# Eighteen unread matrix products behind the last useful one, in five layouts and two widths of weights

## The chip, the core and the metric

The kernel runs on one core of one Trainium2 chip. A core has five engines with instruction streams of their own: PE (TensorE, matrix products into PSUM), DVE (VectorE), ACT (ScalarE), POOL (GpSimd) and SP (SyncE, which here issues most of the DMAs and closes the program). They wait for each other through semaphores. The metric is the device time of one execution in microseconds (us), as the median of some runs.

## The reference

Two blocks follow each other. The first is a linear attention with a polynomial sketch; the second is a feed-forward block with a gate.

```python
phi(x) = outer(S1 @ x, S2 @ x)             # 8 x 8 = 64 features of each token
kv  = sum over s of phi(k) v               # per batch and head
z   = sum over s of phi(k)
x   = (phi(q) @ kv) / (phi(q) @ z + 1e-6)  # 4 batches, 4 heads, 1088 tokens, 32 wide
g   = x @ w_gate                           # x laid out as 4352 tokens x 128
out = (g * sigmoid(g) * (x @ w_val)) @ w_out   # 128 -> 1536 -> 128
```

## The kernel before

The feed-forward block works on transposed tokens: columns are tokens, and the 1536 hidden features are twelve tiles of 128 rows (`j` from 0 to 11). Tokens come in blocks, most of them 480 wide; the last one, `LAST`, is 384 wide and is cut in two for its down projection, 256 columns (`SPLIT`) that go the usual way and 128 that go "straight".

Products in full fp32 are dear on PE, and part of the work is therefore done in *exact parts*. A factor is cut by `cut_weights`, `cut_tokens`, `cut_down` and `cut_hidden` into a high part and a scaled low part that the faster type `float32r` holds without loss; a product of full numbers then becomes three products of parts (L989, L1001 and L1002 for the two up projections, L1069, L1071 and L1072 for the down projection). In the trace a product in full fp32 is two matmul records with a weight load each; a product of exact parts is one. `w_parts[id(wg), 3]` holds the parts of the gate's weights for tiles 9 to 11, and `down_parts["w1"]`, ten tiles of 128 columns, the high parts of the down weights.

PSUM has eight banks of 512 fp32 columns, in one tile `PS`. Single banks are named `g0`, `g1`, `g2` and `acc` (banks 0 to 3), and two pairs `a` (4 and 5) and `b` (6 and 7); `wide("b")` returns the latter pair as a 128 x 2 x 512 view.

The order on each engine is the order in which the code is written; no scheduler moves anything. The main loop goes over the units `(block, j)`: `start_unit` (L989, with an ACT pass at L992), `finish_unit` (L1001, L1002, the activation at L1004, the multiplication on DVE at L1009) and, some units behind, `down`. After the loop PE has left what the last block still owes: the rest of `down` (L1077, in full fp32, negated weights `scaled`) with, in between, twelve `straight` products (L1117, full fp32, 128 x 128, summed in bank 4). Then DVE copies that sum to `o_last` (L1430), and four DMAs, two issued by SP and two by ACT, store it (L1436). Another store, of the other 256 columns (L1141), goes out just before.

What ends the program stands under the line of the function's end, L1462. SP waits there for each DMA queue's last landing and for the engines' last results that it has not yet seen, two semaphores to an instruction; then all engines meet in a barrier, in which POOL collects a signal from each, and in a second one. PE has only its drain and the barrier to do behind its last product.

Of the kernel before, what the change touches and what calls it, by code (L numbers as in the profile page):

```python
# [19 lines left out]
def kernel(  # L20
# [28 lines left out]
    nc = tc.nc  # L49
    P = nc.NUM_PARTITIONS  # L50
# [46 lines left out]
    def touch(*which):  # L97
        for i in which:
            clock[0] += 1
            used[i] = clock[0]  # L100
# [11 lines left out]
    def bank(tag=None):  # L112

        if tag is not None:
            i = place[tag]
        else:
            i = place[free_banks[turn[0] % len(free_banks)]]
            turn[0] += 1
        touch(i)
        return PS[:, i, :]  # L120
# [17 lines left out]
    def wide(tag):  # L138
        i = place[tag]
        touch(i, i + 1)  # L140
        return PS[:, i : i + 2, :]
# [8 lines left out]
    wg = const.tile([P, NCH, P], FP32, name="wg")  # L150
# [84 lines left out]
    def keep_warm(n, w=TB, ps=None):  # L235


        if ps is None:
            ps = bank(free_banks[turn[0] % len(free_banks)])
        for _ in range(n):  # L240
            nc.tensor.matmul(
                ps[0:32, 0:w], warm[:, 0:32], warm[:, 0:w], start=True, stop=True
            )
# [570 lines left out]
    w_parts = {}  # L814
# [76 lines left out]
    down_parts = {}  # L891
# [162 lines left out]
    def down(y=None):  # L1054

        i, j = todo.pop(0)
        n = SPLIT if i == LAST else blocks[i][1]
        first = i not in acc
        if first:
            acc[i] = bank("g2" if i == 1 or i in line[2::2] else "acc")  # L1060
        made[i] = made.get(i, 0) + 1
        mine = [c for c in range(NCH) if (i, c) in DOWN]
        if mine and j == mine[0]:
            acc[i, "p"] = bank("acc" if i in line[2::2] else "g2")
        sides = dict(start=first, stop=(made[i] == NCH))
        if j in mine:
            w1, wb, wd = [down_parts[x][:, FINE.index(j), :] for x in ("w1", "wb", "wd")]
            h1, h0, hd = h_parts.pop((i, j))
            nc.tensor.matmul(acc[i][:, 0:n], wd, hd, **sides)  # L1069
            p = acc[i, "p"][:, 0:n]  # L1070
            nc.tensor.matmul(p, w1, h1, start=(j == mine[0]), stop=False)  # L1071
            nc.tensor.matmul(p, wb, h0, start=False, stop=(j == mine[-1]))  # L1072
            if j == mine[-1]:
                copy_out(y, i, n)
        else:
            w = down_parts["scaled"][:, PLAIN.index(j), :] if mine else wo[:, j, :]
            nc.tensor.matmul(acc[i][:, 0:n], w, hidden[i, j][:, 0:n], **sides)  # L1077
        if i != LAST:
            hidden.pop((i, j))
            slots.append(slot_of[i, j])  # L1080
        if made[i] == NCH:
            if mine:
                put_together(y, i, n)
            elif i == HEAD - 1:

                add_to(behind, 1, lambda: store(i, n))
            else:
                store(i, n)
# [26 lines left out]
    def straight(ps, j):  # L1115

        nc.tensor.matmul(  # L1117
            ps,
            hidden.pop((LAST, j))[:, SPLIT : SPLIT + P],
            wo[:, j, :],  # L1120
            start=(j == 0),
            stop=(j == NCH - 1),
        )
# [3 lines left out]
    def store(i, n):  # L1127
# [7 lines left out]
        while t0 < t1:  # L1135
# [8 lines left out]
                )  # L1144
            t0 += 32 * m

    keep_warm(98, 32)
    keep_warm(12, 64)
    fills = {(w, i): narrow_w(w, i) for w in weights for i in range(len(pieces[w]))}
# [14 lines left out]
    for h in range(H):  # L1164
# [4 lines left out]
            start=True,  # L1169
            stop=True,  # L1170
# [30 lines left out]
    n = steps[0][1]  # L1201
# [95 lines left out]
    w = ("wg", "wv")  # L1297
# [127 lines left out]
    for j in range(NCH):  # L1425
        if todo and j % 4 == 0:
            down()
        straight(ps, j)
    o = fpool.tile([P, D], FP32, name="o_last")
    nc.vector.tensor_copy(o[:], ps)  # L1430
    t0 = blocks[LAST][0] + SPLIT
    b, x0 = divmod(t0 // 32, NX)
# [34 lines left out]
```

## Time and profile before

| | us |
|---|---|
| median of 3 runs (lowest to highest) | 276.84 (276.68 to 276.86) |
| the profiled execution: span from first to last instruction | 275.1 |
| PE busy | 268.8 (98%) |
| VectorE busy | 214.1 (78%) |
| ScalarE busy | 193.6 (70%) |
| GpSimd busy | 105.7 (38%) |
| mean granted TensorE clock | 0.999 |

The profile has no other time of its own execution than the span; what lies around the span, 1.7 us against the median, is the start and the end of an execution outside of the instructions. In a row such as `271.88 0.29 DVE L1430 COPY`, the numbers are the start from the span's beginning and the duration, in us. Records of PE's matmuls overlap, since each holds the time through the array: what a matmul costs its successor is the distance between two starts, not the duration. Rows of groups end in the busy time in us, the mean of one in ns, and the idle time before them.

### The profile page before, as it was taken

To read this page: it belongs to the slowest core of one execution; us is meant where nothing else is said; L and a number is where in the kernel's file an instruction comes from. 1 tells how busy PE (TensorE), PEld (TensorE's weight loads), DVE (VectorE), ACT (ScalarE), POOL (GpSimd) and SP (SyncE) were. 2 spreads that over 40 slices of the span, in tenths; PEclk is the share of its full clock that TensorE was granted. 3 is DMA by queue.
4 is the path that set the end of the run, shared out by engine and by line. 5 is a ranking of instruction groups with operands and counts; after the bars stand their busy time and mean duration, and the time that the engine had idled before them with its cause. 6 is when DMAs were issued, how large, how long until landed. Compare 5 with 4: busy or idle time off the path is not lost.

```text
span 275.1 us, 5788 instructions
## 1 busy us (share of the span) xinstructions
PE 268.8 (98%) x2191; PEld 200.5 (73%) x2191; DVE 214.1 (78%) x373; ACT 193.6 (70%) x349; POOL 105.7 (38%) x117
## 2 busy tenths in 40 slices
PE   7999999999999999999999999999999999999995
PEld 6645566666785786777577777867887888789994
DVE  3997988989788773887545766967987995998871
ACT  2468666462685686677479898769879888897880
POOL 3313422149350640260034353435535663553330
PEclk9999999999999999999999999999999999999999
DMA  6573196122231043000200020000100200010021
GB/s 191 172 216 87 49 270 200 60 104 62 62 88 23 4 111 99 2 0 0 38 12 4 1 38 0 0 2 11 26 2 0 36 1 0 13 25 1 2 36 29
DMA packets 26139, 14.30 MB, mean 52 GB/s; under 512 B 19840, under 2 KB 24192, under 8 KB 26112
## 3 DMA queue, kind: packets, MB, share of 16 engines
q1 hardware_dynamic: 25456, 13.84, 19.6%
q8 instruction: 17, 0.28, 0.4%
q10 hardware_dynamic: 656, 0.10, 0.2%
q14 instruction: 10, 0.08, 0.1%
HBM read 11.41 MB, written 2.23 MB: 50 GB/s over the span
## 4 chain that ended last, share of the span: by engine, by line
PE 93%; DVE 3%; DMA 2%; ACT 1%; issue 0%; SPq 0%
PE PS L1077 20%; PE PS L1001 14%; PE PS L989 14%; PE PS L1002 14%; PE PS L1025 12%; PE PS L1072 3%; PE PS L1071 3%; PE PS L1069 3%; PE PS L354 2%; PE PS L776 2%; PE PS L342 2%; DMA kld<-in_k_dram 2%; PE PS L388 2%; PE PS L1117 1%; PE PS L497 1%; PE PS L445 1%
## 5 line engine op out<-in xcount | busy, mean ns | idle before, releaser
L992 ACT ACTIVATE PS<-PS 128x960 f32<-128x960 f32 (+1 forms) x90 | 83.3, 926 | 29.8 <-PE PS L989 28.8
L1009 DVE SCALAR_TENSOR_TENSOR hbuf<-PS,sg 128x480 f32<-128x480 f32 (+1 forms) x87 | 55.2, 634 | 36.6 <-ACT sg L1004 36.1
L1004 ACT ACTIVATE sg<-PS 128x480 f32<-128x480 f32 (+1 forms) x90 | 49.6, 551 | 1.6 <-PE PS L1002 1.2
L1077 PE MATMUL PS<-hbuf,wo 128*128 128x480 f32 (+2 forms) x94 | 39.4, 516 | 0.0
L989 PE MATMUL PS<-xd,graw 128*128 128x480 f32 (+1 forms) x69 | 37.5, 543 | 0.0
L989 PE MATMUL PS<-xd,wd 128*128 128x480 f32 (+1 forms) x90 | 33.6, 373 | 0.0
L1002 PE MATMUL PS<-x,wb 128*128 128x480 f32 (+1 forms) x90 | 33.5, 372 | 0.0
L1001 PE MATMUL PS<-x,w 128*128 128x480 f32 (+1 forms) x90 | 33.4, 371 | 0.0
L1002 PE MATMUL PS<-x,graw 128*128 128x480 f32 (+1 forms) x69 | 25.5, 370 | 0.0
L989 PEld LDWEIGHTS PS<-xd,wd 128*128 128x128 f32 x90 | 17.0, 189 | 9.9 <-issue 5.3
L1025 PE MATMUL PS<-xT,wg 128*128 128x384 f32 (+1 forms) x60 | 23.5, 473 | 0.1
L1025 PE MATMUL PS<-xT,wv 128*128 128x384 f32 (+1 forms) x60 | 23.2, 467 | 0.3 <-DVE wv L286 0.3
L868 POOL TENSOR_TENSOR x<-xT,x 128x480 fp32r<-128x480 f32 (+1 forms) x6 | 7.2, 1195 | 37.8 <-ACT x L865 37.8
L1077 PEld LDWEIGHTS PS<-hbuf,wo 128*128 128x128 f32 x94 | 17.7, 189 | 5.4 <-issue 0.4
L1029 ACT ACTIVATE sg<-PS 128x384 f32<-128x384 f32 (+1 forms) x24 | 11.2, 468 | 13.2 <-PE PS L1025 12.4
L969 POOL TENSOR_TENSOR hlate<-hbuf,hlate 128x480 fp32r<-128x480 f32 (+1 forms) x12 | 14.6, 1218 | 11.0 <-ACT hlate L968 9.7
L989 PEld LDWEIGHTS PS<-xd,graw 128*128 128x128 f32 x69 | 13.0, 188 | 7.6 <-ACT PS L992 4.1
L1001 PEld LDWEIGHTS PS<-x,w 128*128 128x128 f32 x90 | 16.9, 187 | 2.2
L1002 PEld LDWEIGHTS PS<-x,wb 128*128 128x128 f32 x90 | 16.9, 188 | 2.1
L1001 PE MATMUL PS<-x,graw 128*128 128x480 f32 (+1 forms) x48 | 18.1, 376 | 0.0
L1077 PE MATMUL PS<-hbuf,scaled 128*128 128x480 f32 (+1 forms) x40 | 17.1, 518 | 0.0
L1025 PEld LDWEIGHTS PS<-xT,wv 128*128 128x128 f32 x60 | 11.2, 190 | 7.4 <-DVE hbuf L1040 0.8
(205 smaller groups left out, 572.0 us busy)
## 6 DMA issues: line engine op xcount, KB each, us to landing
kld<-in_k_dram SPq DMA_DIRECT2D x4, 544.0 KB, 4.4
vld<-in_v_dram SPq DMA_DIRECT2D x12, 144.0 KB, 4.3
qld<-in_q_dram SPq DMA_DIRECT2D x3, 544.0 KB, 4.8
raw<-in_moe_w_out_dram SPq DMA_DIRECT2D x4, 384.0 KB, 4.4
raw<-in_moe_w_gate_dram SPq DMA_DIRECT2D x3, 384.0 KB, 3.3
raw<-in_moe_w_val_dram SPq DMA_DIRECT2D x3, 384.0 KB, 3.5
out_dram<-o SPq DMA_DIRECT2D x16, 60.0 KB, 2.0
vld<-in_v_dram SPq DMA_DIRECT2D x4, 112.0 KB, 4.1
```

The lines of the kernel that those rows point to most:

```text
L969: add_to(before, y + 2, lambda: nc.gpsimd.tensor_tensor(out=h0, in0=h, in1=whole(h1), op=ALU.subtract))
L989: nc.tensor.matmul(ps[:, k], w_parts[id(w), j // 3][2][:, j % 3, :], xd, start=True, stop=True)
L992: nc.scalar.activation(ps, ps, AF.Copy, scale=-1.0 / WHOLE)
L1001: nc.tensor.matmul(ps[:, k], w1, x1, start=False, stop=False, skip_group_check=True)
L1002: nc.tensor.matmul(ps[:, k], wb, x0, start=False, stop=True, skip_group_check=True)
L1004: nc.scalar.activation(sg, ps[:, 0], AF.Silu, scale=WHOLE)
L1009: nc.vector.scalar_tensor_tensor(out=hj[:, 0:n], in0=ps[:, 1], scalar=WHOLE, in1=sg, op0=ALU.mult, op1=ALU.mult)
L1025: nc.tensor.matmul(o[:, 0:n], w[:, j, :], xT[:, t0 : t0 + n], start=True, stop=True)
L1029: nc.scalar.activation(sg[:, 0:n], g[:, 0:n], AF.Silu)
L1069: nc.tensor.matmul(acc[i][:, 0:n], wd, hd, **sides)
L1071: nc.tensor.matmul(p, w1, h1, start=(j == mine[0]), stop=False)
L1077: nc.tensor.matmul(acc[i][:, 0:n], w, hidden[i, j][:, 0:n], **sides)
```

## The change

A new function `behind_all` is called between the last `straight` product and the copy to `o_last`. It issues eighteen products of exact parts on PE. The weights are always the high parts of one tile of the gate's weights, the moving operand is always 256 columns out of `down_parts["w1"]`. Each of six views is used three times in a row: the first 256 columns; 256 columns from the second one on; every second one of 512 columns; the first 256 columns taken in steps of 16; the first column 256 times; and again the first 256 columns, with 32 columns of weights in place of 128. The sums alternate between banks 6 and 7, always 256 contiguous columns, and nobody reads them. The output of the kernel is the same.

```diff
+    def behind_all():
+
+        n = 256
+        unread = wide("b")
+        w = w_parts[id(wg), 3][0][:, 0, :]
+        x = down_parts["w1"].rearrange("p c d -> p (c d)")
+        views = [
+            x[:, 0:n],
+            x[:, 1 : n + 1],
+            x[:, 0 : 2 * n].rearrange("p (c t) -> p t c", t=2)[:, 0],
+            x[:, 0:n].rearrange("p (c t) -> p t c", t=16),
+            x[:, 0:1].to_broadcast([P, n]),
+            x[:, 0:n],
+        ]
+        for k, view in enumerate(views):
+            m = 32 if k == 5 else P
+            o = unread[0:m, k % 2, 0:n]
+            if k == 3:
+                o = o.rearrange("p (t c) -> p t c", t=16)
+            for _ in range(3):
+                nc.tensor.matmul(o, w[:, 0:m], view, start=True, stop=True)
 
     keep_warm(98, 32)
     keep_warm(12, 64)
...
         if todo and j % 4 == 0:
             down()
         straight(ps, j)
+    behind_all()
     o = fpool.tile([P, D], FP32, name="o_last")
     nc.vector.tensor_copy(o[:], ps)
     t0 = blocks[LAST][0] + SPLIT
```

## The prediction

> **What bounds the kernel now.** I read the page's first two parts, then the chain that ended last, then the timeline of the last microseconds, and last the instructions of the closing line L1462, by narrow windows.
>
> ```profile
> span 275.1 us, 5788 instructions
> PE 268.8 (98%) x2191; PEld 200.5 (73%) x2191; DVE 214.1 (78%) x373; ACT 193.6 (70%) x349; POOL 105.7 (38%) x117
> PEclk9999999999999999999999999999999999999999
> ```
>
> PE (TensorE) is busy 98% of the span at full granted clock. So work put into its stream before its last useful product would cost its own duration. The change puts work behind that product, so the end has to be read by itself. The chain and the timeline there:
>
> ```profile
> 269.62 0.43 PE PS L1077 x2
> 270.05 1.80 PE PS L1117 x16
> 271.88 0.29 DVE o_last L1430
> ```
> ```profile
> 271.12 0.72 PE L1117 MATMUL PS<-wo,hbuf 128*128 128x128 f32 x5
> 271.88 0.29 DVE L1430 COPY o_last<-PS 128x128 f32<-128x128 f32 x1 [0.88 <-PE PS L1117]
> 272.19 0.80 SPq L1436 DMA_DIRECT2D out_dram<-o_last  x2
> 272.20 0.84 ACTq L1436 DMA_DIRECT2D out_dram<-o_last  x2
> ```
>
> The last product ends at 271.84, VectorE starts its copy 0.04 later, and the four stores are issued until 273.04. From there PE has nothing to do. What the program's end waits for:
>
> ```profile
> DMA to landing us min/median/max: 1.4/1.5/1.6
> L1462 SPq EVENT_SEMAPHORE  x1: 28/28/28, 274.2 to 274.2; - x1
> L1462 PEldq DRAIN  x2: 13/1210/2408, 269.5 to 274.8; - x2
> SPq L1462 <- DMA out_dram<-o_last: 0.8, 2, 0.5
> ```
>
> The first line is of the L1436 stores, the other three are of the closing line. SyncE sits until the stores have landed; the wait that is released last starts at 274.23 (nothing of L1462 stands between 273.95 and 274.23). From there to the end, 275.11, there is only the closing barrier, 0.88 us. PE's first drain, its ticket to that barrier, was over 2.41 us after 269.5, at 271.9. So between 271.84 and about 274.2 PE is free: the cover of this change.
>
> **The change part by part.** Eighteen matmuls with their weight loads are added to PE behind L1117; nothing is removed or moved. In the built order PE has no new wait, VectorE's copy still waits for the twelfth product of L1117 alone, and the DMAs stand as before. One wait is new: SyncE's closing waits now include PE's eighteenth product, sharing an instruction with the landing of a store (the one at 274.23); that splits the eleven waits over one instruction more. The additional one stands first, where SyncE waits for landings anyway: 0 while that cover holds, and one event, some 0.06 by the spacing of these waits, without it. Instruction loading: the page counts 17 blocks, the trace shows about 255 PE instructions between the last blocks and 147 after the last one; 36 more stay inside it, so 0.
>
> Banks 6 and 7 are free and never read. VectorE's copy of bank 4 (0.29) now runs while PE writes other banks, which is also so for every L1009 evacuation: 0; were it to double, the stores would be 0.29 later.
>
> So the only question is when the eighteenth product ends. The plain price, from six such products (exact parts, 256 columns, 128 weights):
>
> ```profile
> 264.10 0.28 PE L1069 MATMUL PS<-hqld,dparts 128*128 128x256 f32 x1
> 264.21 0.28 PE L1071 MATMUL PS<-hkld,dparts 128*128 128x256 f32 x1
> 264.57 0.28 PE L1071 MATMUL PS<-hqld,dparts 128*128 128x256 f32 x1
> 264.69 0.28 PE L1072 MATMUL PS<-hvld,dparts 128*128 128x256 f32 x1
> ```
>
> From 264.10 to 264.69 are five steps: 0.118 each, 0.46 ns a column. The first new product can start 0.112 (the step of L1117) after the last old one started (271.56), at 271.68. All at the plain price: the eighteenth starts 17 x 0.118 = 2.01 later, at 273.69, ends 0.28 later, at 273.97, and its semaphore is seen 0.04 later, at 274.01. That is 0.22 us before 274.23. **Cover left: 0.22 us.**
>
> Layouts, three products each:
> - *Plain, and all from one column (step 0)*: plain price. Step 0 touches less than plain does. Bounds 0.118 and, if a product of exact parts fell back to the price of a full fp32 product, 0.43 (two instructions of 0.215, from six L1077 instructions at 256 columns in 1.29).
> - *Start one column late*: the same contiguous run, 0.118; the same upper bound.
> - *32 weights of 128*: the same columns stream. The sums over ones, L401, use 32 weights and take 379 ns at 256 columns, as L1077 does with 128 weights. So 0.118, upper bound 0.43.
> - *Step 2 and step 16 (8 and 64 bytes between columns)*: no PE row reads with a step. The nearest rows are VectorE's:
>
> ```profile
> L277 DVE SCALAR_TENSOR_TENSOR man<-raw,man 128x384 f32<-128x384 uint32 x10 | 5.5, 549 | 0.0
> L748 DVE TENSOR_TENSOR qab<-qab,den 128x288 f32<-128x288 f32 x3 | 1.4, 457 | 0.1
> L744 DVE TENSOR_REDUCE den<-dot 128x36 f32<-128x288 f32 x3 | 1.4, 453 | 0.1
> L605 DVE TENSOR_REDUCE w<-fold 128x8 f32<-128x64 f32 x3 | 0.8, 276 | 0.1
> L608 DVE TENSOR_TENSOR s<-w,own 128x64 f32<-128x64 f32 x3 | 0.7, 225 | 0.1
> ```
>
> L748 against L608 gives 1.04 ns an element. The contiguous reduce L744 is then 153 + 288 x 1.04. L605 reads its 64 elements 32 bytes apart and needs 276, not 153 + 67 = 220: 1.92 ns each. L277, which reads words 8 bytes apart, goes at (549 - 418)/128 = 1.02. Read together: some 1.9 to 2.0 ns for one visit to a small neighbourhood, and two words from it in the same time. PE's plain row gives 4 x 0.46 = 1.84 ns for four neighbours of 4 bytes, the same size. I take 1.84 ns for each visit: step 16, one column a visit, 256 x 1.84 = 0.471 us; step 2, two columns a visit, 0.236. Bounds: 0.118 for both below (PE hides it); above 256 x 1.92 = 0.49 for step 16, 0.43 for step 2. I take the values near the upper end, since two engines' rows agree on the time of a visit.
>
> Sum: 12 x 0.118 + 3 x 0.236 + 3 x 0.471 = 3.54, against 2.12 plain: 1.41 more, less the cover of 0.22: 1.19 us later. The profiled span of 275.11 becomes 276.30. The median of the runs is 276.84, 1.73 above that span, and I keep that distance: **278.0 us**, 0.4% slower.
>
> [...]
>
> **The rivals.**
> 1. *Not slower: the stores hide it.* PE streams every layout at 0.118 and SyncE's landing wait at 274.23 stays last: 276.84. For it: 0.22 us of cover. Partly so with step 16 at twice the plain price, 0.35 - 0.22 = 0.13: 276.97. It decides until the eighteen together need 0.22 + 0.55 = 0.77 more than 2.12; 0.55 us is the 0.2% that a measurement of this kernel tells from no change. Against it: L605.
> 2. *Only step 16 pays* 0.471: 1.06 - 0.22 = 0.84, 277.68. For it: L277.
> 3. *Products fall back to the full fp32 price*, 0.312 more each. One layout, the 32 weights say: 0.94 - 0.22, 277.56. Late start, step 2 and step 16: 2.81 - 0.22, 279.4. All but plain: 4.68 - 0.22, 281.3. Against: the plain row is all that the trace has of exact parts, and it tells neither way.
> 4. *Faster*: nothing is taken off the chain; no row offers a gain.
>
> **How the numbers follow.** The forecast's mechanism, both steps paying by visits: 0.36. Rival 2: 0.20. Rival 3 in its forms: 0.16. Rival 1: 0.25. Faster: 0.03. The first three are over 0.2%; with some of the mechanism's weaker forms falling under it, slower 0.70, same 0.27. The range reaches from 276.75, which takes in rival 1, to 279.5, rival 3 with three layouts; beyond lie its wider forms, some 0.08, and what is below, about 0.05.
>
> **What the profile of after would show.** Steps of 0.118 between starts for the plain, late-start, step-0 and 32-weight products; 0.236 for step 2 and 0.471 for step 16; the last product's end near 275.4, and SyncE's closing wait put down to PE, not to a store. VectorE's copy and the stores would stand where they are. If the wait stays with the store, rival 1 holds. If another layout has longer steps, rival 3. The prediction is wrong, too, if the end after PE's last product is shorter or longer than the 0.88 us taken here.

## The result, and the profile after

The changed kernel takes 277.00 us against 276.62 before (medians of 20 runs each): 1.0016 times as long, with a 95% interval of 1.0009 to 1.0023. The profiled execution has a span of 275.3 us. The time is 0.4 us more where 1.2 were forecast. The forecast of 278.0 stood on a median of 276.84 for the kernel before, from three runs; the 20 runs have 276.62.

The page, and the chain that ended last, of the changed kernel:

```profile
span 275.3 us, 5825 instructions
PE 271.9 (99%) x2209; PEld 203.2 (74%) x2209; DVE 214.1 (78%) x373; ACT 193.5 (70%) x349; POOL 105.5 (38%) x117
```
```profile
269.85 1.78 PE PS L1117 x16
271.64 2.76 PE PS L1167 x18
```

The eighteen products (L1167) have taken the place of VectorE's copy at the end of the chain, with 2.76 us. The timeline of the same stretch, then what the closing line (L1485 now) waits for:

```profile
271.67 0.29 DVE L1453 COPY o_last<-PS 128x128 f32<-128x128 f32 x1 [0.88 <-PE PS L1117]
271.99 0.80 SPq L1459 DMA_DIRECT2D out_dram<-o_last  x2
272.00 0.84 ACTq L1459 DMA_DIRECT2D out_dram<-o_last  x2
```
```profile
L1485 PEldq DRAIN  x1: 2948/2948/2948, 271.5 to 271.5; - x1
L1485 SPq EVENT_SEMAPHORE  x1: 402/402/402, 274.0 to 274.0; - x1
SPq L1485 <- PE PS L1167: 0.7, 1, 0.7
```

In this execution everything up to the last straight product is 0.20 us earlier than in the profile of before; the copy and the stores keep their distances to it. So the store's landing, which before ended SyncE's wait at 274.23, is due here at 274.03. That is when SyncE's instruction for this store and for PE's last product begins; it then lasts 402 ns, to 274.43, where it took 28 ns before. PE is last, by 0.40 us. What follows the end of that instruction takes 0.86 us in both profiles; the prediction's 0.88 has its 28 ns with it.

What the layouts cost is read from the starts of L1167. The timeline in narrow windows, from the first product with step 2 to the first with step 0 (that last row holds two records, hence x2):

```profile
272.20 0.39 PE L1167 MATMUL PS<-dparts,graw 128*128 128x256 f32 x1
272.41 0.41 PE L1167 MATMUL PS<-dparts,graw 128*128 128x256 f32 x1
272.64 0.41 PE L1167 MATMUL PS<-dparts,graw 128*128 128x256 f32 x1
272.87 0.40 PE L1167 MATMUL PS<-dparts,graw 128*128 128x256 f32 x1
273.09 0.40 PE L1167 MATMUL PS<-dparts,graw 128*128 128x256 f32 x1
273.31 0.40 PE L1167 MATMUL PS<-dparts,graw 128*128 128x256 f32 x1
273.52 0.41 PE L1167 MATMUL PS<-dparts,graw 128*128 128x256 f32 x2
```

Three at step 2: (272.87 - 272.20)/3 = 0.22 us each. Three at step 16: (273.52 - 272.87)/3 = 0.22 each. Forecast were 0.236 and 0.471. The other four layouts start 0.11 to 0.13 after each other, as forecast.

### The profile page after: what moved, and what is told of

The parts are those of the page before. It is cut to its first block, busy times and chain, and to the rows that moved or that the text cites. A ratio compares the mean times of both kernels' runs of the same rounds, so it can differ in the third digit from the quotient of the medians.

```text
span 275.3 us, 5825 instructions
## 1 busy us (share of the span) xinstructions
PE 271.9 (99%) x2209; PEld 203.2 (74%) x2209; DVE 214.1 (78%) x373; ACT 193.5 (70%) x349; POOL 105.5 (38%) x117
## 4 chain that ended last, share of the span: by engine, by line
PE 94%; DVE 3%; DMA 2%; ACT 1%; issue 0%; SPq 0%
PE PS L1077 20%; PE PS L1001 14%; PE PS L989 14%; PE PS L1002 14%; PE PS L1025 12%; PE PS L1072 3%; PE PS L1069 3%; PE PS L1071 3%; PE PS L354 2%; PE PS L776 2%; PE PS L342 2%; PE PS L388 2%; DMA kld<-in_k_dram 2%; PE PS L1167 1%; PE PS L1117 1%; PE PS L497 1%
```

## The experiments

The theory after this reading, A in the expectations: the end goes to the later of the last store's landing and PE's last product, and the two stepped layouts cost 0.22 us a product whatever the step. Two questions remain. Is that all that the change costs? And why does step 16 cost no more than step 2, where VectorE's rows suggested twice as much?

**All eighteen plain.**

```diff
-        views = [
-            x[:, 0:n],
...
-        ]
+        views = [x[:, 0:n]] * 6
...
-            m = 32 if k == 5 else P
+            m = P
```

> All eighteen products read the plain 256 contiguous columns with 128 weights; nothing else differs from the changed kernel. Theory A (the end goes to the later of two, the last store's landing and the last product's end, and only the six stepped products were dear, 0.22 us each in place of 0.12): the eighteen take 18 x 0.119 = 2.14, which ends some 0.2 before the store lands, so the time is that of before, within 0.05 us of it, and the closing wait is put down to the store. Rival B (what the change cost is the added wait in SyncE's closing line or PE's mere presence behind the last product, not the layouts): as slow as the changed kernel, +0.4 us.

Measured: 1.0002 of before (0.9989 to 1.0015). The ratio's interval overlaps that of the changed kernel, so the chain and SyncE's waits have to decide; both of this run:

```profile
271.47 2.17 PE PS L1158 x18
```
```profile
SPq L1476 <- DMA out_dram<-o_last: 0.7, 2, 0.4
L1476 SPq EVENT_SEMAPHORE  x1: 28/28/28, 273.9 to 273.9; - x1
```

No wait is put down to PE. Its last product ends at 273.63, the instruction that waits for the store and for PE begins at 273.86 and takes 28 ns: 0.23 us lie between. In the changed kernel SyncE went on 0.03 us after PE's last product had ended (274.40 to 274.43), so the cover left is 0.20 us, where the prediction had worked out 0.22, with 0.04 for the same signal. SyncE's additional instruction is there as well and costs nothing. Rival B falls.

**All eighteen at step 16.**

```diff
+        views = [x[:, 0:n].rearrange("p (c t) -> p t c", t=16)] * 6
```

> All eighteen products read their columns 64 bytes apart. Theory A, at the 0.219 us between starts that the changed kernel's profile shows: 18 x 0.219 = 3.94 in place of its 2.75, so 1.2 us more than the changed kernel and 1.6 us (0.57%) more than before. Theory of the prediction (0.471 each): 18 x 0.471 = 8.5, 6.1 us more than before. Rival (half of the step's price is a cost of changing from one layout to another, which three in a row hide badly): clearly less than 1.2 us more than the changed kernel.

Measured: 1.0059 (1.0045 to 1.0073), 1.6 us more than before, as theory A has it. The chain and the wait:

```profile
272.00 3.96 PE PS L1159 x18
```
```profile
SPq L1477 <- PE PS L1159: 1.9, 1, 1.9
```

3.96/18 = 0.22 us a product, without any change of layout. Eighteen at 0.471 would have taken 8.5.

**The same eighteen, ahead of the last straight product.**

```diff
     for j in range(NCH):
+        if j == NCH - 1:
+            behind_all()
...
         straight(ps, j)
-    behind_all()
```

> The same eighteen products, issued before the twelfth straight product in place of behind it, so that the copy and the stores wait for all of them. Theory A: they lose their cover and the whole sum, from the changed kernel's starts 12 x 0.119 + 3 x 0.222 + 3 x 0.219 = 2.75 us, is added to before (+1.0%), which makes the cover in the changed kernel 2.75 - 0.4 = 2.35 us. Rival (the products are cheaper than their starts say, and the closing chain behind PE is what grew): less than 2.2 us.

Measured: 1.0102 (1.0088 to 1.0116), 2.8 us. The chain of this run:

```profile
271.81 2.76 PE PS L1167 x18
274.58 0.24 PE PS L1117 x2
```

The products take 2.76 us in both places. Uncovered they cost 2.8, behind the last product 0.4: the stores hide 2.4 us of them.

**Other steps.** From here on each layout is a line of its own with four products, behind the last useful product, and the price is the distance from one line's start to the next, divided by four. Each of these kernels was run once, so only distances inside its profile are compared, not its time.

```diff
+        def step(s, off=0):
+            return every[:, off : off + s * n].rearrange("p (c t) -> p t c", t=s)[:, 0]
+
+        for _ in range(4): nc.tensor.matmul(even, w, every[:, 0:n], **go)
+        for _ in range(4): nc.tensor.matmul(odd, w, step(2), **go)
...
+        for _ in range(4): nc.tensor.matmul(even, w, step(15), **go)
```

> Four products each, in this order: plain; one column in 2, 3, 4, 5, 8 and 15; plain again. Read from the starts in the profile. Half-rate theory (a column outside of a contiguous pair takes twice as long, however far): 0.119 for plain, 0.22 for every step from 2 to 15. Theory of visits to 16-byte neighbourhoods: 0.22 for step 2, and step 4 and above twice that, 0.44. Theory of distance: a rise from step 2 to step 15.

The timeline (steps 2, 3, 4, 5, 8, 15 are L1162 to L1167):

```profile
271.94 1.09 PE L1162 MATMUL PS<-dparts,graw 128*128 128x256 f32 x4
272.86 1.09 PE L1163 MATMUL PS<-dparts,graw 128*128 128x256 f32 x4
273.77 1.11 PE L1164 MATMUL PS<-dparts,graw 128*128 128x256 f32 x4
274.70 1.10 PE L1165 MATMUL PS<-dparts,graw 128*128 128x256 f32 x4
275.62 1.05 PE L1166 MATMUL PS<-dparts,graw 128*128 128x256 f32 x4
276.49 1.15 PE L1167 MATMUL PS<-dparts,graw 128*128 128x256 f32 x4
277.46 0.65 PE L1168 MATMUL PS<-dparts,graw 128*128 128x256 f32 x4
```

0.23, 0.23, 0.23, 0.23, 0.22, 0.24: flat from step 2 on. The theory of distance falls, and so does that of visits to 16-byte neighbourhoods in its simple form. Half rate holds so far.

**Runs of neighbours.**

```diff
+        def runs(length, every_, off=0):
+            m = n // length
+            v = every[:, off : off + every_ * m].rearrange("p (c t) -> p c t", t=every_)
+            return v[:, :, 0:length]
...
+        for _ in range(4): nc.tensor.matmul(of(odd, 2), w, runs(2, 8), **go)
+        for _ in range(4): nc.tensor.matmul(of(even, 2), w, runs(2, 8, 1), **go)
+        for _ in range(4): nc.tensor.matmul(of(odd, 2), w, runs(2, 8, 3), **go)
+        for _ in range(4): nc.tensor.matmul(of(even, 4), w, runs(4, 16), **go)
```

> Four products each, 256 columns, in this order: plain; pairs of neighbours, one pair in every 8 columns, pairs starting at column 0; the same from column 1 (astride two aligned pairs); the same from column 3 (astride two groups of four); fours in every 16; eights in every 32; 128 columns each taken twice; plain. Theory P (PE takes in an aligned pair of columns, 8 bytes, in about 0.87 ns, and a lone column takes as long): plain price 0.119 for the pairs from 0, the fours, the eights and the doubled columns; 0.22 for the pairs from 1 and from 3. Theory Q (a step other than 0 or 1 between neighbouring columns of the pattern halves the rate, whatever lies where): 0.119 for all of them, since all have innermost steps of 1 or 0. Theory R (16-byte groups of four columns, about 0.87 ns each): 0.119 for all but the pairs from 3, which cost 0.22.

```profile
272.00 1.09 PE L1167 MATMUL PS<-dparts,graw 128*128 128x256 f32 x4
272.91 1.11 PE L1168 MATMUL PS<-dparts,graw 128*128 128x256 f32 x4
273.85 1.11 PE L1169 MATMUL PS<-dparts,graw 128*128 128x256 f32 x4
274.78 0.66 PE L1170 MATMUL PS<-dparts,graw 128*128 128x256 f32 x4
275.28 0.64 PE L1171 MATMUL PS<-dparts,graw 128*128 128x256 f32 x4
275.75 0.61 PE L1172 MATMUL PS<-dparts,graw 128*128 128x256 f32 x4
```

All three kinds of pairs cost 0.23, aligned or not; fours and eights 0.12, doubled columns 0.11. All three theories expected something else for the aligned pairs. The pairs from 0 and from 1 have one thing in common with steps of 2: 128 groups of 16 bytes in 0.23 us, 1.8 ns a group. That is the prediction's visit again. Too cheap for it are the columns at steps of 3 (192 groups), those at steps of 4 and more (256) and the pairs from 3, whose two columns lie in different groups (256).

**Other types.** The same bytes as full fp32 and as bf16.

```diff
+        full, short = whole(every), every.bitcast(half)
...
+        for _ in range(4): nc.tensor.matmul(odd, w_full, step(full, 8), **go)
...
+        for _ in range(4): nc.tensor.matmul(odd, w_short, step(short, 16), **go)
```

> Four products each in this order: plain exact parts; full fp32 with contiguous columns, step 2, step 8; bf16 (the same bytes read as 2-byte numbers) with contiguous columns, step 2 (4 bytes), step 4 (8 bytes), step 16 (32 bytes); plain. Theory P (a visit to 8 bytes takes about 0.87 ns): a full fp32 record wants a new column only each 0.87 ns, so all three at 0.215 a record; bf16 0.119 or a little less for contiguous and step 2, 0.22 for steps 4 and 16. Theory Q (any step halves the rate): full fp32 0.43 a record at steps 2 and 8; bf16 0.22 at steps 2, 4 and 16.

Full fp32 at 256 contiguous columns, step 2 and step 8 (two records a product), then bf16 contiguous, step 2, step 4, step 16:

```profile
271.96 1.89 PE L1166 MATMUL PS<-dparts,graw 128*128 128x256 f32 x8
273.69 1.97 PE L1167 MATMUL PS<-dparts,graw 128*128 128x256 f32 x8
275.50 3.85 PE L1168 MATMUL PS<-dparts,graw 128*128 128x256 f32 x8
279.17 0.62 PE L1169 MATMUL PS<-dparts,graw 128*128 128x256 bf16 x4
279.63 0.61 PE L1170 MATMUL PS<-dparts,graw 128*128 128x256 bf16 x4
280.08 1.06 PE L1171 MATMUL PS<-dparts,graw 128*128 128x256 bf16 x4
280.97 2.02 PE L1172 MATMUL PS<-dparts,graw 128*128 128x256 bf16 x4
```

Full fp32: 0.216, 0.226, 0.46 a record. bf16: 0.11, 0.11, 0.22, 0.46; the last from its own row, (2.02 - 0.64)/3, with a record of 0.64. Neither theory P nor Q had this. Visits have it: 256 columns each alone in its 16 bytes take 0.46, 1.8 ns each; two to a group take half; four to a group (bf16, step 2) are free. For these two types the forecast's 0.47 for lone columns is right. Products of exact parts are the exception.

**VectorE's rows, from which the prediction took the visit.** No added products; unread VectorE instructions behind its last copy.

```diff
+    for _ in range(3): nc.vector.tensor_reduce(out=y[:, 0:32], in_=near, axis=AX.X, op=ALU.add)
+    for _ in range(3): nc.vector.tensor_reduce(out=y[:, 0:8], in_=near.rearrange("p i j -> p j i"), axis=AX.X, op=ALU.add)
...
+    for _ in range(3): nc.vector.tensor_tensor(out=y[:, 0:n], in0=step(8), in1=every[:, n : 2 * n], op=ALU.mult)
```

> No added products. Behind VectorE's last copy and the stores, three unread instructions each: a reduce of 64 elements in 8 sums of 8 neighbours; the same 64, each sum over elements 32 bytes apart (the form of L605); 256 elements in 32 sums of 8 neighbours; the same 256 in 8 sums over 32 elements 32 bytes apart; then products of 256 elements with the first operand contiguous, at steps of 8, 16 and 32 bytes. If the prediction read L605 rightly (1.9 ns for each element that lies away from its neighbour): 220 and 276 ns; 419 and 645 ns; 425, 425, 650 and 650 ns. If the surplus of L605 comes from something else than the step: the second and the fourth no dearer than the first and the third by the same ns an element, and the four products alike.

Groups of this run (the reduces of 256 neighbours and of 256 apart, then products with the first operand contiguous and at 8, 16 and 32 bytes):

```profile
L1450 DVE TENSOR_REDUCE unread<-dparts 128x32 f32<-128x256 f32 x3 | 1.3, 420 | 0.1
L1451 DVE TENSOR_REDUCE unread<-dparts 128x8 f32<-128x256 f32 x3 | 1.8, 609 | 0.1
L1452 DVE TENSOR_TENSOR unread<-dparts 128x256 f32<-128x256 f32 x3 | 1.3, 425 | 0.1
L1453 DVE TENSOR_TENSOR unread<-dparts 128x256 f32<-128x256 f32 x3 | 1.3, 425 | 0.1
L1454 DVE TENSOR_TENSOR unread<-dparts 128x256 f32<-128x256 f32 x3 | 1.8, 603 | 0.1
L1455 DVE TENSOR_TENSOR unread<-dparts 128x256 f32<-128x256 f32 x3 | 1.8, 613 | 0.1
```

The small reduces took 216 and 266 ns. Where 645 and 650 ns were expected, 603 to 613 came. The reading of L605 stands in kind: it is the step, from 16 bytes on, at 1.04 + (603 - 425)/256 = 1.74 ns an element (1.92 were taken).

**Weights with a step, and narrow weights with a step in the columns.**

```diff
+        w3 = wide_w.rearrange("p (c t) -> p t c", t=3)[:, 0]
...
+        for _ in range(4): nc.tensor.matmul(even, w3, every[:, 0:n], **go)
+        for _ in range(4): nc.tensor.matmul(odd, w3, every2, **go)
+        for _ in range(4): nc.tensor.matmul(even[0:32], w[:, 0:32], every2, **go)
```

> Four products each in this order: plain; the plain 256 columns with weights taken one column in 3; step 2 in the columns with those weights; step 2 in the columns with 32 weights; plain. If only the moving columns' reads are halved: 0.119, 0.119, 0.22, 0.22, 0.119. If stepped weights load at half rate as well and the load is no longer hidden behind a product of 0.119: the second clearly above 0.119, at up to 0.22, and the third no worse than 0.22. If the narrow product is shortened by its narrower load: the fourth under 0.22.

```profile
271.97 0.85 PE L1163 MATMUL PS<-dparts,graw 128*128 128x256 f32 x4
272.66 1.13 PE L1164 MATMUL PS<-dparts,graw 128*128 128x256 f32 x4
273.60 1.10 PE L1165 MATMUL PS<-dparts,graw 128*32 128x256 f32 x4
274.51 0.66 PE L1166 MATMUL PS<-dparts,graw 128*128 128x256 f32 x4
```

0.17 with stepped weights and contiguous columns (the load's record grows from 190 ns, in the changed kernel's plain products, to 261), 0.23 with both stepped: the two prices do not add up (0.12 + 0.05 + 0.11 would be 0.28). Why they do not is not shown. Narrow weights make a stepped product no cheaper: 0.23.

**Two streams?** The exception of exact parts would follow if PE read their even and odd places side by side, each stream paying 1.8 ns for a change of group: 128 changes in each stream from step 2 on, however far.

```diff
+        for _ in range(4): nc.tensor.matmul(of(odd, 2), w, in_turn(every, 2, 1024), **go)
+        for _ in range(4): nc.tensor.matmul(of(even, 4), w, in_turn(every, 4, 512), **go)
+        for _ in range(4): nc.tensor.matmul(of(odd, 2), w, again(2, 8), **go)
+        for _ in range(4): nc.tensor.matmul(of(even, 4), w, again(4, 8), **go)
+        for _ in range(4): nc.tensor.matmul(of(odd, 4), w, runs(4, 8, 2), **go)
+        for _ in range(4): nc.tensor.matmul(of(even, 6), w, runs(6, 16), **go)
```

> Four products each in this order: (1) plain exact parts; (2) columns taken in turn from two regions, one from each, each region contiguous; (3) in turn from four regions; (4) every eighth column, each twice in a row; (5) every eighth column, each four times; (6) fours in every 8, starting at column 2 (astride two aligned groups of four); (7) sixes in every 16; (8) two regions in turn in full fp32; (9) the same in bf16; (10) plain. Theory T (for exact parts PE reads the even and the odd places of the sequence as two streams side by side, each paying 1.8 ns for each change to another 16-byte group; bf16 and full fp32 have one stream): (2) 0.12, since each stream runs contiguously; (3) 0.23; (4) 0.23; (5) 0.12; (6) 0.23; (7) 2 groups for 3 columns of each stream, 84 x 1.8 = 0.15; (8) and (9) 256 changes, 0.46. Rival cap (one stream at 1.8 ns for a change of group, but never more than 0.23 for a product of exact parts): (2) 0.23, (4) 128 changes, 0.23, (5) 0.12, (6) 0.23, (7) 0.15. Rival half rate (0.9 ns for every change of group): (2) 0.23, (4) 0.12, (6) 0.12, (7) 0.12.

The starts of (2), (3) and (4):

```profile
272.07 0.61 PE L1181 MATMUL PS<-dparts,graw 128*128 128x256 f32 x4
272.51 0.72 PE L1182 MATMUL PS<-dparts,graw 128*128 128x256 f32 x4
273.06 1.09 PE L1183 MATMUL PS<-dparts,graw 128*128 128x256 f32 x4
```

Measured, (2) to (7): 0.11, 0.14, 0.23, 0.12, 0.23, 0.15. Theory T has five of the six, and (2) stands against both rivals. (3) was expected at 0.23 and came at 0.14; (8) and (9), expected at 0.46, came at 0.27 a record and 0.24. Going back and forth between regions was thus cheaper here than stepping on (0.11 and 0.14 against 0.23 in exact parts, 0.27 against 0.46 in full fp32, 0.24 against 0.46 in bf16), and a stream that keeps recent groups could explain (2) without a second stream. So one more run.

**The same columns in another order.**

```diff
+        quad = every[:, 0:1024].rearrange("p (g t c) -> p g c t", t=2, c=8)[:, :, 0:2]
+        pairs = every[:, 0:1024].rearrange("p (g t c) -> p g t c", t=2, c=8)[:, :, :, 0:2]
...
+        for _ in range(4): nc.tensor.matmul(four, w, pairs, **go)
+        for _ in range(4): nc.tensor.matmul(four, w, quad, **go)
```

> Four products each in this order: (1) plain exact parts; (2) pairs of neighbours, one pair in every 8 columns, in the order 0, 1, 8, 9; (3) the very same columns in the order 0, 8, 1, 9; (4) bf16 contiguous; (5) to (8) bf16, in turn from two contiguous runs that lie 16, 64, 512 and 7168 bytes apart; (9) plain. Two streams (even and odd places of the sequence read side by side for exact parts): (2) 0.23 as measured before, (3) 0.12, since each stream then takes both columns of one group before it moves on. One stream that keeps the last few groups at hand and never costs more than 0.23: (2) and (3) alike, 0.23, since the groups are the same. For bf16, where two regions in turn took 0.243 and not 0.46: if the change to a group read shortly before is cheap, (5) to (8) are alike at 0.24; if the distance decides (memory parts that work side by side), the near ones are up to 0.46 and the far ones 0.24.

Pairs, the same columns in the order 0, 8, 1, 9, and contiguous bf16:

```profile
272.10 1.09 PE L1181 MATMUL PS<-dparts,graw 128*128 128x256 f32 x4
273.01 0.63 PE L1182 MATMUL PS<-dparts,graw 128*128 128x256 f32 x4
273.48 0.61 PE L1183 MATMUL PS<-dparts,graw 128*128 128x256 bf16 x4
```

(273.01 - 272.10)/4 = 0.23, and (273.48 - 273.01)/4 = 0.12. The same groups of memory cost half when the even places stay in one group and the odd places in another. One stream with a memory of recent groups can't tell these orders apart; two streams can. How TensorE does it is not shown: two streams is the account that these prices fit, except in turn from four regions, where it expected 0.23 and 0.14 was measured. The bf16 products that go in turn between two runs took 0.24 at all four distances, from 16 to 7168 bytes, so the distance does not decide. Why that is 0.24, and neither 0.11 nor 0.46, stays open.

## Why the prediction was wrong

Its frame held. PE's bound until 271.84, the cover until the store's landing (0.22 forecast, 0.20 measured in the run with eighteen plain products), the closing barrier, nothing for the added wait, for VectorE's copy (0.29 in both profiles) and for instruction loading (17 packets in both): all of it stands in the profiles. So do the plain price (2.17 us for eighteen, 2.12 forecast) and the layouts said to be plain: late start, step 0, 32 weights. Step 2 came at 0.22 instead of 0.236; if exact parts are read as two streams, that is in part luck, since each stream then makes 128 changes of group, as many as the visits that the prediction counted for one.

The step that failed is "step 16, one column a visit, 256 x 1.84 = 0.471 us". It measured 0.22. With that in place the prediction's sum reads 12 x 0.119 + 3 x 0.222 + 3 x 0.219 = 2.75, 0.63 more than the plain 2.12, less 0.22 of cover: 0.41 us. On the 276.62 of these runs that is 277.03; 277.00 was measured. The one term accounts for nearly all of the miss in the added time: 3 x 0.25 = 0.75 of the 0.78 us between the forecast's 1.19 and this 0.41.

The visit of 1.84 ns was no invention. It is 1.8 ns on PE for lone columns in full fp32 and in bf16 (0.46 us for 256), and 1.74 on VectorE. What was wrong was to hand it from other engines and types to products of exact parts without asking whether these read one column at a time. Lone columns cost them 0.9 ns (0.22 us for 256) and not 1.8, as if two places were read side by side. In the trace of before no product on PE reads single columns with a step, in any type, so this could not be read from it. But the prediction did have the bound below (0.118), and rival 1 named "step 16 at twice the plain price", 276.97; that is what happened, with step 2 besides. The two ends for step 16 lay 1.1 us apart, so that choice decided most of the forecast. That VectorE's rows and PE's plain row agree on a size is weaker evidence on a third way of reading than the choice of the value near the upper end says.

Rival 2 (only step 16 pays) and rival 3 (fall back to the price of full fp32) did not happen. What spoke for rival 2, that two words of one neighbourhood cost no more than contiguous ones, holds for VectorE's products (425 ns contiguous and at steps of 8 bytes, 603 at 16) and nearly for full fp32 on PE (0.226 against 0.216). It fails for exact parts (0.23 against 0.12 with two columns to a group, taken in their order) and for bf16 (0.22 against 0.11), where four to a group come at the plain price, 0.11.

## What to carry to other kernels

Work behind TensorE's last useful product was free here only up to the landing of the last store: 2.4 of 2.8 us, and what went beyond, 0.4, was paid in full. On TensorE look at how many columns of a moving operand share 16 bytes. In these runs, for 256 columns, four in one aligned group came at the plain price (0.12 us in exact parts, 0.11 in bf16). Two took twice the time in bf16 (0.22) and, taken in their order, in exact parts (0.23), and 5% more in full fp32 (0.226 a record against 0.216). One alone took four times in bf16 (0.46), twice in exact parts (0.23) and about twice in full fp32 (0.46 a record against 0.216). Before a price is carried over from another engine or type, ask for a row of that very reader and type; where there is none, the price is open between its two ends.

## What the runs showed of the hardware that was not expected

- In products of exact parts the order 0, 1, 8, 9 cost 0.23 us for 256 columns, the order 0, 8, 1, 9 of the same columns 0.12 (e10_order). Two streams, of the even and the odd places, would fit that; no run shows them.
- Contiguous exact parts cost 0.12 us for 256 columns, against 0.11 when each column is used twice (e5_runs), when two regions go in turn (e9_two), and in bf16 (e6_types).
- Weights read one column in three loaded in 261 ns in place of 190, and a product of 256 plain columns then cost 0.17 us in place of 0.12 (e8_sides).
- bf16 columns that alternate between two contiguous runs cost 0.24 us for 256, whether the runs were 16 or 7168 bytes apart (e10_order); lone columns that step on cost 0.46 (e6_types). The cause is open.
